# Retention and gated MLP on one core: w_in loaded by GpSimd with a cast, second w_sg transpose by DMA, state work moved to GpSimd

## The chip, the cores and the metric

The kernel runs on one core of one Trainium2 chip. TensorE (PE) does the matmuls; its weight loads (PEld) overlap them. VectorE (DVE), ScalarE (ACT) and GpSimd (POOL) work element by element, and SyncE (SP) issues DMAs. The metric is the device time of the core in microseconds, as a median of several runs. Most executions of one kernel agree within 0.3%.

## The reference

Eight heads of retention over a batch of 8, a sequence of 576 and a head size of 64, and on their output a gated MLP with a spatial gate:

```python
scores = scale * np.matmul(q, k.transpose(0, 1, 3, 2))
Dmat = np.where(rel >= 0, gamma[:, None, None] ** rel[None, :, :], 0.0)
x = np.matmul(scores * Dmat, v)            # then heads side by side: [8, 576, 512]
h = gelu_tanh(x @ w_in)                    # 512 x 1024
u, v = h[..., :512], h[..., 512:]
v_n = (v - mean(v)) / np.sqrt(var(v) + 1e-06) * g_ln
v_s = np.einsum('ts,bsd->btd', w_sg, v_n) + b_sg[None, :, None]
out = x + (u * v_s) @ w_out
```

Inputs and output are float32; the kernel's matmuls are in bfloat16.

## The kernel before, in words

Two batch rows of 576 positions make nine tiles of 128; four such pairs make N = 36 units. A unit is 256 positions of four heads, or, for the middle one of each nine (MID), 64 positions of both rows and all heads. For a unit, q, k and v are loaded (`load`, L288 and L280), scaled by powers of gamma and cast (`transposed`: q L484, k L478 or L480, v L487), q and k are transposed on PE (L500) or, from unit 24, by DMA, and copied out as qkT (L503). The scores (`score`, L525) are masked with a triangle on DVE (`mask`, L539, table `tri`), and multiplied with v (`outp`, L638).

Instead of scores over the whole past, a state of each head is carried. `states` (L558) makes the products of k and v of a unit's two chunks; `keep` copies them from PSUM (L585), adds the first chunk to the state (s1, L607, DVE), the second (s2, L614, DVE), and spreads both over the diagonal blocks of zbdB (L611, ACT) and zbdA (L590, POOL in the first four units, then DVE). `outp` multiplies those with q (L630). Up to unit 8 (JOIN) a unit's states and scores are an instruction group of their own, which takes the PSUM tile "oz"; after that they are joined with the output of the unit before. PSUM has the pools "tp", "s", "oz" and "d", the last with three banks that the MLP's products, the transposes of w_sg and the filler matmuls share.

The MLP follows the units: `mlp_V` (L702) the v half with w_in, then gelu (L705), statistics on DVE (L710 to L712), the power of -1/2 on POOL (L715), and the normalised tile vn (L727, ACT). `mlp_U` (L742) is the u half, transposed. When a batch row's tiles are complete, `batch` multiplies vn with the transposed w_sg (L764), gates on DVE (L772), multiplies by w_out (L784), adds x on PE (L787), and stores (L791, L793). The transposed w_sg exists twice, as wT0 for even rows of the batch and wT1 for odd ones, whose rows are shifted by half a tile. Free rows of their half-filled tiles carry b_sg, and those of vmid 1/g, split into two bfloat16 each (`g_and_b`).

Weights: w_in goes by SP in four loads of float32 into `wst`, and ACT casts it in eight pieces (`w_load`, L301, L305). w_sg is cast by POOL (L419), transposed on PE ten times (L428) and copied out by DVE and ACT (L437, L435). w_out is loaded (L443) and scaled by g on DVE (L446).

The order of the work is computed when the program is built. Every piece is added with `plan.add(engine, cost, key, ...)`; for each engine, the class `Plan` emits of the pieces that are ready by its own reckoning the one with the smallest key. A key is a due time (unit number times T0 = 5300) plus a correction from the table SHIFT, by engine, name of the tile and stage. On the chip each engine and each DMA queue then runs its list in that order, each piece behind its semaphores. Where PE would be idle in the first 45 us of that reckoning, `fill` puts in matmuls with zeros (L267).

Of the kernel before, what the change touches and what calls it, by code (L numbers as in the profile page):

```python
# [11 lines left out]
F32 = mybir.dt.float32  # L12
# [14 lines left out]
    "ACT xT late": 9412, "ACT xT mid": -23216, "ACT zbd late": -5690, "ACT zbd mid": 6227, "ACT zbdB e1": 8971,  # L27
    "ACT zbdB e2": 3443, "ACT zbdB e3": -2224, "ACT zbdB e5": 3662, "ACT zbdB e6": 1034, "ACT zbdB late": -8232,
    "ACT zbdB mid": 2910, "ACT zc e0": -5530, "ACT zc e2": -2593, "ACT zc e3": -15140, "ACT zc e6": 4358,
    "ACT zc late": 1898, "ACT zc mid": 4282, "ACT zmid e4": -40267, "ACT zmid late": 5855, "DVE b_rows e-2": 20418,  # L30
    "DVE b_rows e2": 8415, "DVE dtab e-2": -10349, "DVE gT e6": -9934, "DVE gT late": 4844, "DVE gT mid": -35727,
    "DVE g_col1 e2": 31456, "DVE g_rows e-2": -2310, "DVE qkT e0": 1726, "DVE qkT e1": 7061, "DVE qkT e3": 13460,
    "DVE qkT e4": -10701, "DVE qkT e5": -9864, "DVE qkT e6": -228, "DVE qkT late": 9156, "DVE qkT mid": 18488,
    "DVE qs e0": -234, "DVE qs e1": 24362, "DVE qs e3": 6022, "DVE ret e0": 703, "DVE ret e1": 1576,
    "DVE ret e2": 5275, "DVE ret e3": 8812, "DVE ret e4": 3411, "DVE ret e6": 6523, "DVE ret late": 7318,
# [5 lines left out]
    "DVE st3 e6": 1761, "DVE st3 late": -8207, "DVE st3 mid": -22642, "DVE vmid_g e2": 6581, "DVE wT e3": -5068,  # L41
    "DVE wT e5": -5845, "DVE wT_b e2": -3449, "DVE w_out e3": -15568, "DVE w_out e5": 25437, "DVE zbdA e4": -1133,
    "DVE zbdA e5": -5539, "DVE zbdA e6": -14755, "DVE zbdA late": -198, "DVE zbdA mid": -2512,
# [809 lines left out]
```

## Time and profile before

| | |
|---|---|
| median of 3 runs | 225.62 us (225.03 to 226.07) |
| profiled execution | 225.79 us |
| its span, first to last instruction | 223.4 us |
| mean granted TensorE clock | 0.998 |
| busy: PE, PEld | 206.5 us (92%), 143.4 us (64%) |
| busy: DVE, ACT, POOL | 172.6 us (77%), 156.3 us (70%), 120.0 us (54%) |
| DMA | 45.86 MB, mean 205 GB/s |
| matmuls with zeros (L267) | 36, 12.4 us |

Busy time counts matmuls of the filler too. An average over the span hides that the kernel has stages: an opening in which inputs and weights arrive, a long middle, and a tail in which the last outputs are made. A DMA share of 1 means that the 16 DMA engines always had packets under way. POOL's 54% hold long waits, since its list is in a fixed order.

### The profile page before, as it was taken

The page shows a single profiled execution, that of the slowest core. Times are in us where ns is not written, and L with a number is a line of the kernel's source. Part 1 is how long each engine was busy: PE and PEld are TensorE (multiplying, and loading weights), DVE is VectorE, ACT ScalarE, POOL GpSimd, SP SyncE. Part 2 cuts the span into 40 slices and gives each one's busy share as a digit, 9 for nine tenths or more (in the row PEclk, how much of TensorE's full clock was granted, in tenths as well). Part 3 has the DMA queues.
Part 4 walks back from the last instruction along what each step waited for, and adds up shares of the span by engine and source line. Part 5 has one row for each costly group of instructions (what it writes and reads, how often), then busy time and mean ns, then how long its engine had stood idle before and what let it go on. Part 6 is the DMA issues. An engine that isn't in the chain of part 4 may idle for free.

```text
span 223.4 us, 7695 instructions
## 1 busy us (share of the span) xinstructions
PE 206.5 (92%) x3085; PEld 143.4 (64%) x3122; DVE 172.6 (77%) x424; ACT 156.3 (70%) x351; POOL 120.0 (54%) x160
## 2 busy tenths in 40 slices
PE   4997879999998899999999998999989999999993
PEld 1454457677675676677767775677656766676751
DVE  5888587899998998769988997769889677665420
ACT  5276996936687558798577666895887678847432
POOL 4273559894788667485556476656767341002000
PEclk9999999999999999999999999999999999999999
DMA  4999899999899976879756999999889158300324
GB/s 91 284 311 188 260 285 308 269 335 294 176 293 305 321 196 179 243 216 301 242 147 208 229 200 198 221 264 204 218 186 224 53 50 175 112 1 0 144 94 188
DMA packets 84674, 45.86 MB, mean 205 GB/s; under 512 B 28768, under 2 KB 77920, under 8 KB 84640
## 3 DMA queue, kind: packets, MB, share of 16 engines
q1 hardware_dynamic: 84640, 45.38, 79.2%
q8 instruction: 24, 0.39, 0.8%
q14 instruction: 10, 0.08, 0.1%
HBM read 32.79 MB, written 9.44 MB: 189 GB/s over the span
## 4 chain that ended last, share of the span: by engine, by line
PE 68%; DVE 12%; DMA 7%; POOL 4%; ACT 4%; issue 3%; POOLq 0%; ACTq 0%
PE p_d L764 13%; PE p_d L784 12%; PE p_d L742 11%; PE p_d L702 10%; DMA qkf<-in_q_dram 6%; PE p_oz L638 4%; PE p_tp L500 3%; PE p_d L787 3%; PE p_s L525 3%; PE p_d L267 3%; DVE ret L539 2%; PE p_oz L630 2%; PE p_oz L558 2%; DVE s L607 2%; ACT xT L667 2%
## 5 line engine op out<-in xcount | busy, mean ns | idle before, releaser
L715 POOL TENSOR_TENSOR stat<-stat,mhalf 128x1 f32<-128x1 f32 x36 | 20.2, 561 | 55.0 <-DVE stat L712 45.0
L539 DVE TENSOR_TENSOR ret<-p_s,tri 128x512 bf16<-128x512 f32 x64 | 42.3, 684 | 8.1 <-PE p_s L525 8.1
L487 POOL TENSOR_TENSOR vb<-vf,gv 128x512 bf16<-128x512 f32 x36 | 39.0, 1084 | 9.8 <-DMA vf<-in_v_dram 6.5
L764 PE MATMUL p_d<-wT,vn 128*128 128x288 bf16 x256 | 41.1, 286 | 0.6 <-ACT vn L727 0.6
L742 PE MATMUL p_d<-xT,w_in 128*128 128x256 bf16 (+1 forms) x320 | 37.5, 262 | 2.0 <-ACT xT L667 1.9
L484 POOL TENSOR_TENSOR qkb<-qkf,gq 128x512 bf16<-128x512 f32 x32 | 34.7, 1085 | 5.2 <-issue 4.9
L727 ACT ACTIVATE vn<-vg,stat 128x512 bf16<-128x512 f32 x32 | 25.9, 812 | 16.3 <-DVE stat L717 15.8
L702 PE MATMUL p_d<-w_in,xT 128*128 128x512 bf16 x121 | 34.7, 380 | 2.6 <-ACT xT L667 0.8
L784 PE MATMUL p_d<-w_out,uT 128*128 128x512 bf16 x133 | 36.2, 379 | 0.7 <-issue 0.2
L772 DVE TENSOR_TENSOR uT<-p_d,uT 128x288 bf16<-128x288 f32 x64 | 28.4, 450 | 6.8 <-PE p_d L764 6.4
L742 PEld LDWEIGHTS <-w_in 128*128 128x128 bf16 x320 | 28.0, 98 | 8.3 <-issue 2.5
L710 DVE BATCH_NORM_STATS2 stat<-vg 128x6 f32<-128x512 f32 x36 | 24.7, 686 | 9.8 <-ACT vg L705 9.6
L764 PEld LDWEIGHTS <-vn 128*128 128x128 bf16 x256 | 24.5, 98 | 9.4 <-issue 1.1
L791 ACT ACTIVATE ob<-p_d 128x512 f32<-128x512 f32 x36 | 21.2, 593 | 12.7 <-PE p_d L787 11.9
L667 ACT ACTIVATE xT<-p_oz 128x256 bf16<-128x256 f32 x64 | 24.4, 456 | 4.9 <-PE p_d L742 2.6
L747 ACT ACTIVATE uT<-p_d 128x512 bf16<-128x512 f32 x36 | 21.5, 597 | 7.9 <-PE p_d L742 7.5
L480 POOL CAST qkb<-qkf 128x512 bf16<-128x512 f32 x32 | 21.1, 660 | 9.7 <-issue 4.2
L705 ACT ACTIVATE vg<-p_d 128x512 f32<-128x512 f32 x36 | 21.3, 593 | 4.5 <-PE p_d L702 3.9
L702 PEld LDWEIGHTS <-xT 128*128 128x128 bf16 x144 | 12.5, 98 | 12.1 <-ACT xT L667 1.3
L784 PEld LDWEIGHTS <-uT 128*128 128x128 bf16 x144 | 13.3, 98 | 10.5
L764 PE MATMUL p_d<-wT,vmid 128*128 128x288 bf16 x64 | 18.3, 286 | 0.8 <-DVE uT L772 0.8
L611 ACT ACTIVATE zbdB<-s 64x128 bf16<-64x128 f32 x48 | 14.7, 306 | 6.2 <-DVE s L607 5.5
(87 smaller groups left out, 322.5 us busy)
## 6 DMA issues: line engine op xcount, KB each, us to landing
out_dram<-ob SPq DMA_DIRECT2D x36, 256.0 KB, 3.2
qkf<-in_q_dram SPq DMA_DIRECT2D x32, 256.0 KB, 5.0
qkf<-in_k_dram SPq DMA_DIRECT2D x32, 256.0 KB, 5.1
vf<-in_v_dram SPq DMA_DIRECT2D x32, 256.0 KB, 5.1
wst<-in_moe_w_in_dram SPq DMA_DIRECT2D x4, 512.0 KB, 5.8
wsg<-in_moe_w_sg_dram SPq DMA_DIRECT2D x4, 288.0 KB, 7.2
qkf<-in_q_dram SPq DMA_DIRECT2D x8, 128.0 KB, 5.1
qkf<-in_k_dram SPq DMA_DIRECT2D x8, 128.0 KB, 4.8
```

Source lines behind the costliest of these rows:

```text
L484: plan.add("DVE" if soon else "POOL", 640 if soon else 1030, key, lambda: eng.tensor_tensor(split(qs[a]), shape(qkf[l][:, 0, :]), gain(gq) ...
L487: plan.add("POOL", 1030, key + 2, lambda: nc.gpsimd.tensor_tensor(shape(vb[a][:]), shape(vf[l][:]), gain(gv), op=Alu.mult), reads=rd(i, 2) ...
L539: nc.vector.tensor_tensor(ret[r][hh][:].rearrange("p (s k j) -> p s k j", s=2, k=2), banks[0][:].rearrange("p (s k) j -> p s k j", s=2), t ...
L667: nc.scalar.activation(xT[p % NX][:, 2 * c:2 * c + 2, 128 * (m + e):128 * (m + e) + 128].rearrange("p k (j s) -> p k s j", s=2), oz[:, e, ...
L702: nc.tensor.matmul(banks[0][:], xT[p % NX][:, kk, 128 * m:128 * m + 128], w_in[:, kk, F2:], start=(kk == 0), stop=(kk == KK - 1))
L710: nc.vector.bn_stats(st[:, 0:6], vg[g][:])
L727: nc.scalar.activation(vn[p % 2][m][:], vg[g][:], Act.Identity, scale=st[:, 8:9], bias=st[:, 9:10])
L742: nc.tensor.matmul(hu[:, c, :], w_in[:, kk, 128 * (x * per + c):128 * (x * per + c) + 128], xT[p % NX][:, kk, cols], start=(kk == 0), stop ...
L747: plan.add("ACT", 500, key, lambda banks, x=x: nc.scalar.activation(uT[p % NX][:, x * per:x * per + per, cols], banks[0][:].rearrange("p ( ...
L764: nc.tensor.matmul(banks[0][:, :HS], src[:, 128 * c:128 * c + 128], wT[e][j][:, half * HS:(half + 1) * HS], start=(j == 0), stop=(j == SB ...
L772: plan.add("DVE", 370, key, lambda banks, c=c, col=col: nc.vector.tensor_tensor(uT[x][:, c, col:col + HS], banks[0][:, :HS], uT[x][:, c, c ...
L784: nc.tensor.matmul(banks[0][:], uT[x][:, c, r], w_out[:, c, :], start=(c == 0), stop=False, skip_group_check=True)
```

## The change

- **w_in**: `w_load` now issues four DMAs from GpSimd's queue that cast on the way and write the bfloat16 tile. Two stand behind vb of unit 0, the v half's, two behind vb of unit 1. The four loads on SP, the staging tiles (two are left, for w_out) and ACT's eight casts go.
- **g and b**: their three small loads and the work on them get later keys. GpSimd's constants are split: the ramp first, the identity, then the triangle (`pool_c`), on which the masks now wait instead of on the identity.
- **wT1**: PE transposes w_sg once, five tiles with five evacuations; wT1 is filled by two DMAs in SBUF, half the partitions each, from wT0, after all five tiles. The second batch row's products wait on them.
- **State**: s2 and all of zbdA but that of MID go to POOL. w_out is scaled on POOL too.
- **PSUM**: up to unit 8 the states take banks of "d", two where both chunks have a state, instead of "oz", and ACT copies each bank out by itself.
- **SHIFT** has new values throughout, so the order of the pieces changes in many places. In the planner a DMA of another engine than SP no longer holds that engine until the transfers before it are done.

```diff
@@ Plan.emit
             if dma:
-                free[e] = max(t + cost, pipe - 1000)
+                if e == "SP":
+                    free[e] = max(t + cost, pipe - 1000)
@@ w_load
-    def w_load(half, c, s):
-        plan.add("SP", 600, (-0.4 - 0.2 * half) * T0 + c,
-                 lambda: nc.sync.dma_start(wst[s][:], moe_w_in.rearrange("(c p) f -> p c f", p=128)
-                                           [:, c:c + 2, half * F2:(half + 1) * F2]),
-                 writes=[("wst", s)], dma=1900)
-        for r in range(2):
-            plan.add("ACT", 500, (1 + 0.4 * (1 - half)) * T0, lambda r=r: nc.scalar.activation(
-                w_in[:, c + r, half * F2:(half + 1) * F2], wst[s][:, r, :], Act.Copy),
-                reads=[("wst", s)], writes=[("w_in", half, c + r)])
+    def w_load(half, c):
+        plan.add("POOL", 900, (1 - half) * T0 + 10 + c, lambda: nc.gpsimd.dma_start(
+            w_in[:, c:c + 2, half * F2:(half + 1) * F2],
+            moe_w_in.rearrange("(c p) f -> p c f", p=128)[:, c:c + 2, half * F2:(half + 1) * F2]),
+            reads=[("vb", 1 - half)], writes=[("w_in", half, c), ("w_in", half, c + 1)], dma=1500)
@@ tables
-        plan.add("POOL", 200, early, pool_a, writes=["srow_i"])
-        plan.add("POOL", 1000, early + 1, pool_b, writes=["ident"])
+        plan.add("POOL", 350, early, pool_a, writes=["srow_i"])
+        plan.add("POOL", 600, early + 1e6, pool_b, writes=["ident"])
+        plan.add("POOL", 1500, early + 2e6, pool_c, writes=["tri"])
@@ g_and_b
-        plan.add("SP", 600, early + 1, lambda: nc.sync.dma_start(
+        plan.add("SP", 600, -2.9 * T0, lambda: nc.sync.dma_start(
             g_col[:], moe_g_ln.rearrange("(c p) -> p c", p=128)), writes=["g_col"], dma=300)
...
-        plan.add("SP", 900, early + 1, b_load, writes=["b_col"], dma=300)
+        plan.add("SP", 900, -2.9 * T0 + 1, b_load, writes=["b_col"], dma=300)
...
-        low = 2 * T0
+        low = 3 * T0
@@ weights
-        for e in range(2):
-            for j in range(SB):
...
+        for j in range(SB):
...
+        for x in range(2):
+            plan.add("SP", 600, kw + 2 * T0, lambda x=x: nc.sync.dma_start(
+                wTs[1][NB0:, :, :] if x == 0 else wTs[1][:NB0, 1:, :],
+                wTs[0][:NB0, :, :] if x == 0 else wTs[0][NB0:, :SB - 1, :]),
+                reads=[("wT", 0, j) for j in range(SB)], writes=[("wT1", x)], dma=1100)
...
-                plan.add("DVE", 450, kw + 1 * T0, lambda c=c, s=s, r=r: nc.vector.tensor_scalar(
+                plan.add("POOL", 620, kw + 1 * T0, lambda c=c, s=s, r=r: nc.gpsimd.tensor_scalar(
                     w_out[:, c + r, :], wst[s][:, r, :], g_col[:, c + r:c + r + 1], None, op0=Alu.mult),
@@ keep
+                for e, b in enumerate(banks):
+                    nc.scalar.activation(z[:, e].rearrange("p k d -> p (k d)"), b[:, :2 * D], Act.Copy)
...
-            plan.add("DVE", 220, key + 5, lambda: nc.vector.tensor_tensor(s2[c][:], z[:, 1], mid, op=Alu.add),
+            plan.add("POOL", 300, key + 5, lambda: nc.gpsimd.tensor_tensor(s2[c][:], z[:, 1], mid, op=Alu.add),
                      reads=[name, mid_name], writes=[("s2", c)])
             v = int(n > 1)
-            build("POOL" if i < 4 else "DVE", ("zbdA", c, v), zbdA[c][v], s2[c][:], [("s2", c)])
+            build("POOL", ("zbdA", c, v), zbdA[c][v], s2[c][:], [("s2", c)])
@@ attention
             def run(banks):
-                states(i, banks[0], 0, True)
-                score(i, banks[1:])
+                states(i, [banks[0], banks[w - 1]], True)
+                score(i, banks[w:])
             u = plan.add("PE", 470 if i % U == MID else 590, i * T0 + 3, run, reads=[("qkT", i % NR), ("kb", a), ("vb", a)],
-                         writes=[("sc", i), ("z", i)], take=[("oz", 1), ("s", 2)])
+                         writes=[("sc", i), ("z", i)], take=[("d", w), ("s", 2)])
@@ the order in which the pieces are added
-    for n, (half, c) in enumerate(((1, 0), (1, 2), (0, 0), (0, 2))):
-        w_load(half, c, n)
...
         attention(i)
+        if i < 2:
+            for c in (0, 2):
+                w_load(1 - i, c)
```

More of the change, by code (lines that the diff above doesn't have):

```diff
@@ L60 @@
-    "POOL zbdB late": 2130, "POOL zbdB mid": -3212, "SP b_col e-2": 12547, "SP g_col e-2": -9283,
-    "SP ld e0": -3117, "SP ld e1": -4642, "SP ld e2": 5103, "SP ld e3": -172, "SP ld e5": -1411, "SP ld e6": 5603,
-    "SP ld late": 11669, "SP ld mid": 1614, "SP out late": 2815, "SP out mid": 11693, "SP qkT late": -2778,
-    "SP qkT mid": -127, "SP wo e0": 24367, "SP wo e5": 3300, "SP wo e6": -1941, "SP wsg e0": -1456,
-    "SP wsg e1": 3613, "SP wsg e3": -5539, "SP wsg e4": -18215, "SP wst e-1": -392,
[7 rows of a table added]
@@ new lines @@
+    "POOL s2 e6": -10518, "POOL s2 late": -954, "POOL s2 mid": 4265, "POOL srow_i e-2": -24929, "POOL st2 e2": 765,
[3 rows of a table added]
+    "POOL w_in e0": 828, "POOL w_in e1": 4002, "POOL w_out e5": -4332, "POOL wnat e2": 6035, "POOL wnat e4": 6803,
+    "POOL zbdA e0": -1437, "POOL zbdA e1": -8927, "POOL zbdA e2": -5148, "POOL zbdA e3": -1976,
+    "POOL zbdA e5": -6423, "POOL zbdA e6": 3401, "POOL zbdA late": -4447, "POOL zbdA mid": -4628,
+    "POOL zbdB e0": 5300, "POOL zbdB e1": 93, "POOL zbdB e2": 4275, "POOL zbdB e5": -773, "POOL zbdB late": 2130,
[6 rows of a table added]
@@ L238 @@
     ob = [sb(f"ob{i}", [128, DM], F32) for i in range(NO)]
-    wst = [sb(f"wst{i}", [128, 2, F2], F32) for i in range(4)]
+    wst = [sb(f"wst{i}", [128, 2, F2], F32) for i in range(2)]
     w_in = sb("w_in", [128, KK, 2 * F2])
@@ new lines, in weights, with tr, put @@
+        for j in range(SB):
+            n = min(128, S - 128 * j)
+            def tr(banks, j=j, n=n):
+                for t in range(SB):
+                    w = min(128, S - 128 * t)
+                    nc.tensor.transpose(banks[0][:].bitcast(BF)[:n, 128 * t:128 * t + w],
+                                        wnat[:w, t, 128 * j:128 * j + n], ident[:w, :w])
+            u = plan.add("PE", 290, kw + 1 * T0, tr, reads=[("wnat", t) for t in range(SB)] + ["ident"],
+                         writes=[("wTp", j)], take=[("d", 1)])
+            def put(banks, j=j, n=n):
+                dst, src = wT[0][j][:n, :], banks[0][:].bitcast(BF)[:n, :S]
+                if j % 2:
+                    nc.scalar.activation(dst, src, Act.Copy)
+                else:
+                    nc.vector.tensor_copy(dst, src)
+            plan.add("ACT" if j % 2 else "DVE", 520 if j % 2 else 385, kw + 1 * T0, put,
+                     reads=[("wTp", j)], writes=[("wT", 0, j)], give=[(u, [0])])
@@ L641, in run @@
             if joined:
-                states(i + 1, oz, 2 * 128, False)
+                states(i + 1, [oz[:, e, 256:] for e in range(2)], False)
                 score(i + 1, banks[1:])
```

93 lines of the change are left out of this document (42 added, 51 removed), and 56 rows, old and new, of the table SHIFT.

## The prediction

> **What bounds the kernel now.** I read the page's head first, then busy time by stretch, then the same for the filler matmuls (L267), which do no work of the kernel. Columns: bounds in us, length, busy us (instructions) of PE, PEld, DVE, ACT, POOL, granted clock, DMA share, GB/s.
>
> ```profile
> span 223.4 us, 7695 instructions
> 0.00:20.00 20.00, 15.80 (x200) 7.93 (x204) 15.73 (x46) 10.29 (x35) 8.65 (x21) 1.00 0.94 233
> 20.00:35.00 15.00, 12.40 (x182) 7.69 (x182) 10.89 (x28) 14.01 (x28) 8.89 (x13) 1.00 0.91 253
> 35.00:45.00 10.00, 9.42 (x169) 6.85 (x168) 7.84 (x17) 8.46 (x17) 8.76 (x13) 1.00 1.04 279
> 45.00:80.00 35.00, 33.02 (x559) 24.28 (x563) 33.47 (x78) 23.14 (x56) 25.81 (x32) 1.00 1.06 289
> 80.00:210.00 130.00, 126.23 (x1913) 90.60 (x1936) 101.88 (x252) 96.82 (x212) 67.90 (x86) 1.00 0.72 174
> 210.00:223.40 13.40, 9.64 (x73) 6.08 (x72) 2.81 (x7) 3.58 (x6) 0.00 (x0) 0.96 0.38 144
> ```
> The fillers alone:
> ```profile
> 0.00:20.00 20.00, 9.70 (x27) 3.05 (x31) 1.00 0.94 233
> 20.00:35.00 15.00, 2.73 (x11) 0.61 (x8) 1.00 0.91 253
> ```
> PE's useful work is 6.1 us of the first 20, 9.7 of the next 15 and 9.4 of the next 10. From 80 to 210 us PE is busy 97%: there it is the bound, and little can be won but by giving it less to do. So the time is PE's work plus what PE loses: 13.9 us in 0:20, 5.3 in 20:35, 0.6 in 35:45, 2.0 in 45:80, 3.8 in 80:210, 3.8 in the tail. The change acts on the first three, and in 45:80, where DVE (96%), PE (94%) and the DMA engines are all near full at once.
>
> The opening by timeline (start, length):
> ```profile
> 0.80 0.45 SPq L362 DMA_DIRECT2D g_col<-in_moe_g_ln_dram  x1
> 1.31 0.49 SPq L367 DMA_DIRECT2D b_col<-in_moe_b_sg_dram  x1
> 1.85 0.56 SPq L368 DMA_DIRECT2D b_col<-in_moe_b_sg_dram  x1
> 2.46 0.58 SPq L288 DMA_DIRECT2D qkf<-in_q_dram  x1
> ...
> 11.82 1.34 SPq L301 DMA_DIRECT2D wst<-in_moe_w_in_dram  x2
> ...
> 13.72 1.38 POOL L487 TENSOR_TENSOR vb<-vf,gv 128x512 bf16<-128x512 f32 x1
> ...
> 16.37 5.58 SPq L280 DMA_DIRECT2D vf<-in_v_dram  x2
> 16.70 0.76 ACT L667 ACTIVATE xT<-p_oz 128x256 bf16<-128x256 f32 x2 [0.50 <-PE p_oz L638]
> ...
> 22.00 1.14 SPq L301 DMA_DIRECT2D wst<-in_moe_w_in_dram  x2
> 22.75 1.67 PE L702 MATMUL p_d<-w_in,xT 128*128 128x512 bf16 x7 [0.16 <-issue]
> ...
> 30.21 1.14 ACT L305 ACTIVATE w_in<-wst 128x512 bf16<-128x512 f32 x2
> 31.84 1.91 PE L742 MATMUL p_d<-xT,w_in 128*128 128x256 bf16 x16
> ```
> The first q load is the fourth DMA. xT of the first pair of units is there at 17.46, but the v half's matmuls (L702) begin at 22.75 and the u half's (L742) at 31.84, right behind ACT's casts of w_in. ACT is busy 14.01 of 15 us there. The MLP could have filled PE, and w_in was late.
>
> **The change, part by part.** Prices by shape (count | busy us, mean ns | idle before):
> ```profile
> L590 DVE TENSOR_TENSOR zbdA<-s,blk 128x256 bf16<-128x256 f32 x20 | 10.9, 546 | 0.3
> L590 POOL TENSOR_TENSOR zbdA<-s,blk 128x256 bf16<-128x256 f32 x4 | 2.7, 670 | 6.2 <-DVE s L614 6.2
> L614 DVE TENSOR_TENSOR s<-zc,s 128x128 f32<-128x128 f32 x16 | 8.3, 520 | 0.2
> L614 DVE TENSOR_TENSOR s<-zc 128x128 f32<-128x128 f32 x8 | 3.9, 492 | 0.0
> L484 POOL TENSOR_TENSOR qkb<-qkf,gq 128x512 bf16<-128x512 f32 x32 | 34.7, 1085 | 5.2 <-issue 4.9 <-DMA qkf<-in_q_dram 0.3
> L480 POOL CAST qkb<-qkf 128x512 bf16<-128x512 f32 x32 | 21.1, 660 | 9.7 <-issue 4.2 <-POOL stat L715 3.3 <-POOL qkb L484 2.2
> L446 DVE TENSOR_SCALAR w_out<-wst,g_col 128x512 bf16<-128x512 f32 x4 | 2.3, 596 | 0.0
> L305 ACT ACTIVATE w_in<-wst 128x512 bf16<-128x512 f32 x8 | 4.6, 619 | 0.0
> L585 ACT ACTIVATE zc<-p_oz 128x256 f32<-128x256 f32 x24 | 9.0, 374 | 3.0 <-PE p_oz L558 2.9
> L585 ACT ACTIVATE zc<-p_oz 128x128 f32<-128x128 f32 x8 | 2.2, 276 | 1.2 <-PE p_oz L558 1.1
> ```
>
> (a) Second transposed w_sg by DMA. Half of L428's transposes go. Their windows:
> ```profile
> 35.00:45.00 10.00, 4.72 (x49) 3.39 (x49) 1.00 1.04 279
> sum 45.00, PE 4.94 PEld 3.48; mean PE 2.47 PEld 1.74
> ```
> 25 of 50 leave PE: 2.5 us, in a stretch where PE has hardly a gap, so I count all of it. Five evacuations on DVE and ACT go too. Added are two copies in SBUF, 64 partitions each: 64 x 5 x 1152 B and 64 x 4 x 1152 B, 0.66 MB, which at the 289 GB/s of 45:80 is 2.3 us of DMA time in a full stretch. Batch 1 is their reader, some two units after batch 0, so their landing is covered; without that cover they cost a landing:
> ```profile
> vf<-in_v_dram SPq DMA_DIRECT2D x32, 256.0 KB, 5.1
> ```
> 5.1 us for a load. The two issues stand in SP's queue behind the wait for all five tiles; the loads queued behind wait with them. Bounds: 0 (fewer loads then needed at once) and 4.6 us (only half the partitions are written at a time, half rate). I take 1.2, nearer to the lower, because units are loaded up to five ahead.
>
> (b) g and b later. The first load moves from 2.46 to 0.80, 1.66 us, and everything that the DMA engines pace until 20 us moves with it (share 0.94). Bounds 0 and 1.66, the whole, since nothing else stands ahead of it; I take 1.7. The three issues (1.5 us) now stand between loads of SP's queue, where a pair of issues takes up to 5.58 us for lack of room; hidden there, else 1.5. GpSimd's ramp constant goes first and its triangle last; DVE's eight copies for g and b leave the way of the first q and land after 16 us, where 20:35 has 4.1 us of DVE idle: nothing either way.
>
> (c) w_in by four casting loads. ACT loses eight casts, 4.6 us, in its fullest stretch, and w_in no longer waits for them. The loads go out behind vb of units 0 and 1, some 8 to 11 us, ahead of where 11.82 and 22.00 were. PE lost 5.3 us in 20:35, so the gain is between 0 and 5.3, and I take half, 2.7: half a w_in (1.05 MB, 3.6 us at 289 GB/s) now flows beside the q, k and v of units 2 to 4 that used to flow after them, and delays those. POOL issues four DMAs: no row of before shows one. The nearest are SP's, 0.67 us for a w_in load (1.34 for two) and 2.8 for a blocked one: 2.7 to 11 us of POOL, the lower nearest as the rings are empty then; POOL is busy 8.65 of the first 20, which hides it. Behind them on POOL wait vb of unit 1 and zbdA; if uncovered they delay unit 1 by 1.3 us.
>
> (d) States into the "d" banks for units 0 to 8. PE does the same matmuls; ACT's one copy of 374 ns becomes two of 276 in six of them: 6 x 0.18 = 1.1 us, paid from the 4.6 it gains. What is late next: two of three "d" banks are held until those copies end, while "oz" is free for the output. Bounds: five units that meet MLP work x 0.55 = 2.8 lost, 0.37 x 5 = 1.9 won. I take 0.
>
> (e) s2, zbdA and w_out from DVE to POOL. DVE loses 8.3 + 3.9 + 10.9 + 2.3 = 25.4 us of 172.6. POOL gains 20 x 0.67 = 13.4; for s2 (128x128, no row) the line through 670 ns at 256 and 1085 at 512 columns gives 0.46, bounds 0.25 and 0.67, so 24 x 0.46 = 11.0; w_out has one streamed input, so nearer to the cast's 0.66 than to 1.09: 2.6 to 4.3. In 45:80:
> ```profile
> 45.00:80.00 35.00, 2.54 (x5) 1.00 1.06 289
> 45.00:80.00 35.00, 3.41 (x5) 0.00 (x0) 1.00 1.06 289
> ```
> Five L614 and five L590 by window: DVE falls by 2.54 + 3.41 + 2.30 = 8.3 to 25.2 of 35, POOL rises by 5 x 1.13 + 2.6 = 8.3 to 34.1. DVE's fullness goes and POOL's takes its place. PE lost 2.0 us there; I take neither gain nor loss, since the state products are wanted only two units later. The bounds are 2.0 won and the second rival's loss.
>
> The row has POOL at 670 ns against DVE's 546 for the same zbdA. The Trainium skill (GPSIMD Engine Reference, Engine selection) holds GpSimd to be about twice as slow for two-input elementwise work. By that, an estimate from DVE's rows, the ten products and sums would cost 5 x 2 x (0.55 + 0.51) = 10.6 instead of 5.7 us and POOL would need 39 of 35 us; the sum would come out near 224, the second rival's time. The four POOL rows speak against it, at 1.2 times.
>
> Sum against the profiled execution's 225.79 (span 223.40 and 2.39 around it): 2.5 - 1.2 + 1.7 + 2.7 = 5.7, so 220.1. That execution stands 0.17 over the median of 225.62; I say 220.0. Half a per cent, 1.1 us, is about what a measurement of this kernel can tell from no change, as its runs spread from 225.03 to 226.07.
>
> **The rivals.**
> First: the opening speeds up more. w_in early also brings statistics, gelu and batch 0 forward. PE loses 19.8 us before 45; with all of (b), all 5.3 of 20:35 and no price for the copies: 225.8 - 2.5 - 1.7 - 5.3 = 216.3. For it: POOL idles 11 of the first 20 us and ACT is freed. Against: the DMA share is 0.91 to 1.06 from the start, so loads cannot come much sooner.
>
> Second: POOL becomes the bound in 45:80. At 34.1 of 35 us it has no room for its waits:
> ```profile
> POOL stat L715 <- DVE stat L712: 45.0, 24, 9.0
> ```
> It waits 45 us over the run for DVE's statistics, in order, with q, k and v of later units queued behind, whose buffers gate SP's loads. If half of the 9.2 us it idles there cannot be used, 8.3 - 4.6 = 3.7 us goes on the path: 223.7. Against: DVE, which it waits for, becomes quicker.
>
> Third, slower: w_in starves the first units. The casting loads sit ahead of units 2 to 4 in the DMA engines. If a casting transfer holds them twice as long as a plain one (no row shows one), 2.1 MB costs 7.3 us more, before the MLP has anything to cover it: 227.3. It decides from 5.7 us extra, 1.8 times the plain transfer; slower by over half a per cent from 6.8. For it: share 0.94 in 0:20. Against: the transfer writes half the bytes. The Trainium skill (DMA: Bandwidth & Descriptors, Issuing engines are not separate DMA queues) says that queues of all engines end on the same 16 DMA engines and interleave; no run here has a second queue yet.
>
> Fourth: the change doesn't bite. DMA paces PE until 45 whatever is removed, the copies in SBUF eat what the transposes gave: 225.5.
>
> **How the numbers follow.** Forecast (217.5 to 222.5) 0.47; first rival 0.13; second 0.15; fourth 0.08; third 0.17. Faster: 0.47 + 0.13 + 0.15 = 0.75; within half a per cent 0.08; slower 0.17. The range reaches from the first rival's 216 to 225.5: it leaves out 0.17 and a little of the first rival.
>
> **What would show it.** (a) PE's transposes at 25, no evacuation into the second wT. (b) First q issue near 0.8. (c) L702's successor before 20 us and L742's before 26, fillers under 12.4 us (9.70 + 2.73); wrong if vb of unit 2 (POOL, 13.72 before) begins more than 3 us later. (d) No wait of PE for ACT's zc copies over a microsecond. (e) DVE under 150 us, POOL near 150; wrong if PE's lost time in 45:80 grows over 2 us. The whole fails if PE's useful work by 45 us stays near 25 us.

## The result, and the profile after

The changed kernel takes 230.40 us in the median (four runs, 230.32 to 231.16) beside 225.32 us for the kernel before (four runs, 224.21 to 226.07): a ratio of 1.0247, 95% interval 1.0213 to 1.0281. It is slower by 5.1 us, where 220.0 was forecast with a range to 225.5. The profiled execution took 230.45 us, with a span of 228.6. Ratios, here and below, leave out executions in the chip's slower state; medians are of all executions.

Line numbers of the changed kernel: L275 filler, L392 the subtraction in `b_split`, L412 its transposes on PE, L308 the casting loads of w_in, L458 w_out's scaling, L634 s2, L610 the diagonal blocks zbdA, L722 and L762 the v and u halves of the MLP, L784 the spatial products, L804 the output products.

Busy time by stretch after the change, with the columns of the prediction's first table, and below it the fillers alone:

```profile
0.00:20.00 20.00, 15.31 (x193) 7.37 (x193) 13.78 (x34) 11.27 (x38) 11.82 (x27) 1.00 1.03 231
20.00:35.00 15.00, 9.03 (x153) 5.69 (x155) 14.06 (x28) 6.60 (x17) 10.44 (x14) 0.86 0.82 224
35.00:45.00 10.00, 9.89 (x129) 7.10 (x130) 5.87 (x17) 7.51 (x13) 6.68 (x10) 0.88 1.02 255
45.00:80.00 35.00, 32.04 (x554) 23.19 (x554) 25.54 (x58) 23.90 (x60) 34.63 (x44) 1.00 0.91 230
80.00:210.00 130.00, 125.88 (x1957) 89.38 (x1955) 94.28 (x230) 97.60 (x211) 85.01 (x119) 1.00 0.78 187
210.00:228.60 18.60, 14.70 (x113) 9.34 (x110) 3.88 (x9) 6.67 (x11) 0.32 (x1) 1.00 0.38 142
```
```profile
0.00:20.00 20.00, 8.52 (x23) 2.34 (x23) 0.27 (x1) 1.00 1.03 231
20.00:35.00 15.00, 1.20 (x4) 0.27 (x4) 0.00 (x0) 0.86 0.82 224
```

PE's useful work by 45 us is 15.31 + 9.03 + 9.89 - 9.72 = 24.5 us, against 25.2 before: the sign that the prediction had named for its failure as a whole. And a part of those 24.5 us ran at a lower clock (0.86 and 0.88 instead of 1.00), so still less was done in them. POOL stands at 34.63 of 35 us in 45:80, and PE's lost time there grew from 2.0 to 3.0 us; DVE is busy 157.4 us, where under 150 was named. So two of the signs for (e) failed as well. The chain of work that ended last, in order of time (start, length, what), names three places:

```profile
27.52 4.40 DVE b_rows L392
...
55.66 1.55 POOL w_out L458
...
60.44 3.09 POOL w_out L458 x2
...
83.75 3.28 DVE zbdA L610 x2
```

**The first place, 27 to 37 us.** The timeline (start, length) of DVE, POOL and PE there:

```profile
27.25 0.23 DVE L391 CAST b_rows<-b_col 128x8 bf16<-128x8 f32 x1
27.52 4.39 DVE L392 TENSOR_TENSOR b_rows<-b_col,b_rows 128x8 bf16<-128x8 f32 x1
31.94 0.17 DVE L393 COPY b_rows<-b_rows 128x16 bf16<-128x16 bf16 x1
```
```profile
27.00 0.45 POOL L634 TENSOR_TENSOR s<-zc,s 128x128 f32<-128x128 f32 x1
27.39 0.66 POOL L426 CAST wnat<-wsg 64x576 bf16<-64x576 f32 x1
28.02 0.66 POOL L610 TENSOR_TENSOR zbdA<-s,blk 128x256 bf16<-128x256 f32 x1
28.64 1.05 POOL L496 TENSOR_TENSOR qkb<-qkf,gq 128x512 bf16<-128x512 f32 x1
29.64 0.60 POOL L492 CAST qkb<-qkf 128x512 bf16<-128x512 f32 x1
30.21 1.05 POOL L499 TENSOR_TENSOR vb<-vf,gv 128x512 bf16<-128x512 f32 x1
31.21 0.66 POOL L426 CAST wnat<-wsg 128x576 bf16<-128x576 f32 x1
```
```profile
27.44 0.29 PE L537 MATMUL p_s<-qkT 64*64 64x64 bf16 x14
32.17 0.77 PE L412 MATMUL p_d<-ident,b_rows 128*128 128x128 bf16 x5 [4.44 <-DVE b_rows L391]
```

A subtraction of eight columns, 0.18 us in the kernel before (at 5.28 us, with nothing beside it), is on DVE for 4.39 us: from 27.52 to 31.91 us, while POOL works through six instructions without a gap and ends at 31.87. PE's next instructions in order need b's rows and wait 4.44 us. An instruction of the moved work for g was held as well, though no wait of PE shows for it: L365, 0.16 us in the kernel before, is on DVE for 1.60 us, from 13.66 to 15.26, and POOL's run of work ends at 15.23. What follows is PE's clock (four-microsecond stretches; the clock is the third number from the end):

```profile
28.00:32.00 4.00, 0.00 (x0) 0.00 (x0) 3.97 (x2) 0.53 (x2) 3.87 (x6) 0.83 0.99 286
32.00:36.00 4.00, 3.83 (x33) 2.14 (x34) 3.30 (x11) 1.19 (x2) 0.00 (x0) 0.50 1.12 318
36.00:40.00 4.00, 4.00 (x33) 2.59 (x32) 1.48 (x7) 1.79 (x3) 1.77 (x3) 0.81 1.03 248
```

PE is busy 7.83 of the 8 us after the stop, at a clock of 0.50 and 0.81. In the kernel before it is 1.00 throughout the first 45 us. The Trainium skill (TensorE: Matmul & The Clock Gate, Part 1) has PE fall to half clock after an idle window of about 3.4 us; the 4.44 us here agree. In e_fill, below, it falls after a shorter stop too.

**The second place, 54 to 64 us.** Groups by shape (count | busy us, mean ns of one | idle before):

```profile
L458 POOL TENSOR_SCALAR w_out<-wst,g_col 128x512 bf16<-128x512 f32 x4 | 6.2, 1565 | 0.0
L492 POOL CAST qkb<-qkf 128x512 bf16<-128x512 f32 x32 | 19.4, 606 | 1.3 <-PE p_s L537 1.1 <-PE p_oz L570 0.2
L610 POOL TENSOR_TENSOR zbdA<-s,blk 128x256 bf16<-128x256 f32 x24 | 16.5, 687 | 0.4
L634 POOL TENSOR_TENSOR s<-zc 128x128 f32<-128x128 f32 x8 | 3.6, 452 | 0.3 <-ACT zc L601 0.2
L804 PE MATMUL p_d<-w_out,uT 128*128 128x512 bf16 x144 | 37.2, 379 | 2.2 <-POOL w_out L458 2.2
```

One scaling of w_out takes 1.57 us on POOL, 2.6 times DVE's 0.60 and 2.6 times a cast of the same shape on POOL. The four stand between q, k and v of later units, POOL has no room left, and PE waits 2.2 us for them.

**The third, at 83.75 us,** is DVE's pair of products of the middle unit. It takes 3.36 us from 83.66 us, beside POOL instructions without a gap until 86.41; the same pair takes 0.74 us at 33.14, where POOL stands still. PE waits 1.65 us behind it. So of the chain, 12.3 us stand in these three.

The rest of the opening went as forecast: the transposes (L433) are 25, the first q load is issued at 0.79 us, the v half begins at 14.23 instead of 22.75 us and the u half at 19.79 instead of 31.84. Only the fourth unit is later: its v lands at 20.7 instead of 16.2 us, with the casting loads of w_in under way from 7.4 to 20.9 us, and is prepared 7 us later (L499 at 23.38 instead of 16.33 us).

### The profile page after: what moved, and what is told of

It is laid out like the page before. It is cut to its first block, busy times and chain, and to the rows that moved or that the text cites. A ratio compares the mean times of both kernels' runs of the same rounds, so it can differ in the third digit from the quotient of the medians.

```text
span 228.6 us, 7635 instructions
## 1 busy us (share of the span) xinstructions
PE 206.8 (90%) x3085; PEld 142.1 (62%) x3085; DVE 157.4 (69%) x373; ACT 153.6 (67%) x347; POOL 148.9 (65%) x212
## 3 DMA queue, kind: packets, MB, share of 16 engines
q0 software_dynamic: 1088, 1.05, 2.8%
## 4 chain that ended last, share of the span: by engine, by line
PE 49%; DVE 19%; ACT 10%; POOL 9%; DMA 7%; issue 3%; SPq 0%; ACTq 0%; POOLq 0%
PE p_d L784 12%; PE p_d L722 9%; PE p_d L804 9%; PE p_d L762 8%; DVE ret L551 5%; DMA w_in<-in_moe_w_in_dram 4%; DVE stat L730 3%; PE p_oz L658 3%; POOL vb L499 2%; PE p_d L807 2%; DVE s L627 2%; ACT vg L725 2%; POOL w_out L458 2%; DVE zbdA L610 2%; DVE b_rows L392 2%
## 5 line engine op out<-in xcount | busy, mean ns | idle before, releaser
L499 POOL TENSOR_TENSOR vb<-vf,gv 128x512 bf16<-128x512 f32 x36 | 38.2, 1064 | 11.2 <-PE p_oz L658 8.1
L784 PE MATMUL p_d<-wT,vn 128*128 128x288 bf16 x256 | 41.0, 286 | 1.0 <-ACT wT L441 0.5
L762 PE MATMUL p_d<-xT,w_in 128*128 128x256 bf16 (+1 forms) x320 | 38.6, 266 | 2.3 <-DMA w_in<-in_moe_w_in_dram 0.8
L722 PE MATMUL p_d<-w_in,xT 128*128 128x512 bf16 x144 | 37.9, 388 | 3.0 <-DMA w_in<-in_moe_w_in_dram 1.9
L804 PE MATMUL p_d<-w_out,uT 128*128 128x512 bf16 x144 | 37.2, 379 | 2.2 <-POOL w_out L458 2.2
L496 POOL TENSOR_TENSOR qkb<-qkf,gq 128x512 bf16<-128x512 f32 x32 | 33.9, 1060 | 1.7 <-PE p_tp L512 1.3
L762 PEld LDWEIGHTS <-w_in 128*128 128x128 bf16 x320 | 28.4, 99 | 8.0 <-issue 2.1
L784 PEld LDWEIGHTS <-vn 128*128 128x128 bf16 x256 | 24.1, 98 | 10.5 <-issue 3.6
L687 ACT ACTIVATE xT<-p_oz 128x256 bf16<-128x256 f32 x64 | 24.5, 459 | 5.0 <-PE p_oz L658 3.9
L722 PEld LDWEIGHTS <-xT 128*128 128x128 bf16 x144 | 14.0, 100 | 14.3 <-issue 4.5
L804 PEld LDWEIGHTS <-uT 128*128 128x128 bf16 x144 | 12.8, 98 | 13.0 <-issue 2.6
L492 POOL CAST qkb<-qkf 128x512 bf16<-128x512 f32 x32 | 19.4, 606 | 1.3 <-PE p_s L537 1.1
L784 PE MATMUL p_d<-wT,vmid 128*128 128x288 bf16 x64 | 18.4, 287 | 1.7 <-DVE uT L792 1.7
```

The costliest lines, as they stand in the source:

```text
L496: plan.add("DVE" if soon else "POOL", 640 if soon else 1030, key, lambda: eng.tensor_tensor(split(qs[a]), shape(qkf[l][:, 0, :]), gain(gq) ...
L499: plan.add("POOL", 1030, key + 2, lambda: nc.gpsimd.tensor_tensor(shape(vb[a][:]), shape(vf[l][:]), gain(gv), op=Alu.mult), reads=rd(i, 2) ...
L687: nc.scalar.activation(xT[p % NX][:, 2 * c:2 * c + 2, 128 * (m + e):128 * (m + e) + 128].rearrange("p k (j s) -> p k s j", s=2), oz[:, e, ...
L722: nc.tensor.matmul(banks[0][:], xT[p % NX][:, kk, 128 * m:128 * m + 128], w_in[:, kk, F2:], start=(kk == 0), stop=(kk == KK - 1))
L762: nc.tensor.matmul(hu[:, c, :], w_in[:, kk, 128 * (x * per + c):128 * (x * per + c) + 128], xT[p % NX][:, kk, cols], start=(kk == 0), stop ...
L784: nc.tensor.matmul(banks[0][:, :HS], src[:, 128 * c:128 * c + 128], wT[e][j][:, half * HS:(half + 1) * HS], start=(j == 0), stop=(j == SB ...
```

## The experiments

Each keeps the order of the kernel it starts from, but for what it moves, unless "planned anew" stands beside it. Ratios are against the kernel before on the same chip; one per cent is 2.26 us. A difference of two ratios is good to about 0.6 to 1 per cent, since executions spread wider than the 0.3% named at the start: those of the kernel before from 224.07 to 227.66 us on one chip.

| run | median us | ratio to the kernel before, 95% interval |
|---|---|---|
| the changed kernel | 230.40 | 1.0247 [1.0213, 1.0281] |
| e_brow | 229.12 | 1.0121 [1.0058, 1.0185] |
| e_fill | 229.08 | 1.0129 [1.0082, 1.0177] |
| e_wout | 226.68 | 1.0055 [1.0022, 1.0087] |
| e_state | 233.73 | 1.0361 [1.0308, 1.0413] |
| e_brow_wout | 225.42 | 0.9986 [0.9951, 1.0022] |
| e_brow_wout_mid | 221.76 | 0.9838 [0.9779, 0.9897] |
| e_undo_b | 229.57 | 1.0185 [1.0134, 1.0235] |
| e_undo_c (planned anew) | 229.51 | 1.0195 [1.0142, 1.0248] |
| e_wnat_act | 228.14 | 1.0157 [1.0104, 1.0209] |
| e_best_undo_b | 221.34 | 0.9861 [0.9808, 0.9914] |
| e_best_undo_c (planned anew) | 224.05 | 0.9937 [0.9898, 0.9977] |
| e_best_undo_a (planned anew) | 228.35 | 1.0139 [1.0092, 1.0186] |
| e_best_again | 221.37 | 0.9817 [0.9733, 0.9901] |
| e_best_undo_a2 | 228.99 | 1.0107 [1.0023, 1.0191] |
| e_best_state | 229.92 | 1.0165 [1.0101, 1.0229] |
| e_best_wnat | 219.80 | 0.9729 [0.9668, 0.9790] |

The theory at the start: two separate losses, DVE's moved work held beside POOL (and PE's clock with it), and w_out on POOL. Rivals: one loss seen from two sides; w_in landing late; the state work on POOL. In the expectations, theory A is the held work, B is POOL's fullness from 45 to 80 us, and C is w_in landing late.

### The held subtraction: e_brow, e_fill

e_brow does b's subtraction on POOL, in its place:

```diff
-                    nc.vector.tensor_tensor(lo, x, hi, op=Alu.subtract)
+                    nc.gpsimd.tensor_tensor(lo, x, hi, op=Alu.subtract)
```

> The changed kernel with one edit: the subtraction that makes b's second bfloat16 part (L392, two inputs in SBUF) runs on POOL instead of DVE; the order on PE, ACT and SP is the same. Theory A, the lock: DVE's L392 took 4389 ns for work of some 180 because POOL ran without a gap from 27.0 to 31.9 us, PE had nothing for 4.4 us, and then a granted clock of 0.5 for about 5 us. Without it PE's gap at 28 us goes, the clock stays at 1.0, and the kernel takes 224 to 226 us (4.4 us of gap and up to 2 of slow clock). Theory B, POOL is the bound from 45 to 80 us: the opening's gain is taken back there, 228.5 to 230.5 us. Theory C, w_in lands late and holds the third unit: the gap is another wait in disguise, PE stands still at 28 us all the same, 229.5 to 230.5 us.

It took 0.21 us there, so its data had been in place. The ratio falls by 1.26 points, 2.8 us; the time, 229.12, lies in the range of theory B and above that of A. In the trace its gelus and outputs lead the changed kernel's by 1.0 us at 17 us, before the edit acts, by up to 5.8 us at 38 and by a constant 3.0 to 3.2 from 56 us on. The clock is 1.00 from 28 us on, and the 4.4 us stop is gone. But the hold itself went to the next DVE instruction with two inputs in SBUF:

```profile
29.57 3.70 DVE L610 TENSOR_TENSOR zbdA<-zmid,blk 128x256 bf16<-128x256 f32 x2
```
```profile
34.26 1.02 PE L722 MATMUL p_d<-w_in,xT 128*128 128x512 bf16 x4 [1.84 <-DVE wT L417]
```

e_fill keeps the hold and has PE do eleven matmuls with zeros in the gap:

```diff
         def b_tr(banks):
+            for _ in range(11):
+                fill(banks[0])
```

> The changed kernel with 11 filler matmuls of 379 ns ahead of the transposes of b on PE, where it stood still for 4.4 us. The wait stays, only the clock after it is kept up. Theory A: the slow clock has a price of its own; matmuls from 32 to 37 us run at 1.0 instead of 0.5, 1.5 to 2.5 us saved, 228 to 229 us. If the clock's drop has no price (other engines set the pace after the wait): 230 to 230.8 us. Theory B: no change either, 230 us.

PE's gap fell to 1.96 us, but the clock, which was to stay up, fell all the same: 0.57 in 32:36, with 1.00 in the stretches on either side. The trace's lead over the changed kernel was 0.7 us at 23 us, before the edit acts, 1.4 at 57 us and within 0.3 of nought from 67 us on; the median is 1.3 us lower, with runs from 227.86 to 230.31. The lead goes where the clock falls a second time: 0.70 in 64:68, behind two waits for w_out of 1.1 and 1.2 us, where the changed kernel has the same waits and 1.00. So the run doesn't give the clock a price of its own.

### w_out on POOL: e_wout, and both together: e_brow_wout

```diff
-                plan.add("POOL", 620, kw + 1 * T0, lambda c=c, s=s, r=r: nc.gpsimd.tensor_scalar(
+                plan.add("POOL", 620, kw + 1 * T0, lambda c=c, s=s, r=r: nc.vector.tensor_scalar(
                     w_out[:, c + r, :], wst[s][:, r, :], g_col[:, c + r:c + r + 1], None, op0=Alu.mult),
```

> The changed kernel with the four scalings of w_out back on DVE (596 ns each there before, 1565 ns on POOL now), at the same places of the order. Theory B: POOL, at 34.6 of 35 us in 45 to 80, gets 6.3 us back and PE does not wait 2.2 us for w_out at 62 us; 225.5 to 228 us. Theory A: the loss lies before 45 us and POOL's queue catches up later; 229.5 to 230.5 us.

1.92 points, 4.3 us. The lag against the changed kernel is nought to 60 us, -2 at 65 to 80 and -3.5 from 89 us on: the second and, POOL having room, the third place. One scaling took 0.69 us on DVE, in the mean.

> Both single undos at once: the subtraction of b on GpSimd and the four scalings of w_out back on DVE, the order on PE, ACT and SP as in the changed kernel. If the two are separate losses they add: 3.0 + 3.5 = 6.5 us off, about 224.0, half a per cent under the kernel before. If they are one loss seen from two sides (the opening's lag is caught up wherever GpSimd has room again), no more than the larger, 3.5 us, comes off: 226.9. If w_in's late landing holds the opening by itself, the same 226.9 and the lag against the changed kernel stays near nought until 60 us.

2.61 points, 5.9 us, where the two alone gave 2.8 and 4.3. The time lies between the cases for one loss (226.9) and for two (224.0), and the points are nearer to the sum than to the larger, within their doubt: so two losses for the most part. The version without them is level with the kernel before, and no better.

### The last hold: e_brow_wout_mid

The middle unit's products go to POOL as well:

```diff
-            e = nc.gpsimd if eng == "POOL" else nc.vector
+            e = nc.gpsimd
```

> The same, and the middle unit's two zbdA products (DVE, at 29.6 us held for 3.70 instead of 0.9) on GpSimd as well. If a DVE instruction is held only because it is of the kind that GpSimd's back-to-back work keeps out, the next one of that kind takes its place and nothing is won (224.0, give or take 0.5). If the two products were the last in the way, PE's 1.84 us at 34 us goes and a lock at 84 us with it: 222.0 to 223.0. Price: 1.4 us more on GpSimd per middle unit.

Another 1.5 points, 3.3 us: 221.76, and 221.37 when run again (e_best_again). No DVE instruction is longer than 1.7 us from 10 to 95 us, and in the profiled execution the clock is 1.00 in every stretch of the opening. The holds and w_out together cost the changed kernel 9.2 us by the ratios, 10.0 us by the traces' ends. Without them the change is faster than the kernel before by 1.6 to 1.8 per cent.

> The fastest version once more, to stand beside the three below: 221.8, within 1.2 us.

### Taking away what DVE waits for: e_wnat_act

Instead of moving the held instruction, five casts are taken from POOL:

```diff
-            plan.add("POOL", 575, kw, lambda j=j, n=n: nc.gpsimd.tensor_copy(wnat[:n, j, :], wsg[j][:n, :]), reads=[("wsg", j)], writes=[("wnat", j)])
+            plan.add("POOL", 575, kw, lambda j=j, n=n: nc.scalar.activation(wnat[:n, j, :], wsg[j][:n, :], Act.Copy), reads=[("wsg", j)], writes=[("wnat", j)])
```

> The changed kernel with the five float32-to-bfloat16 casts of w_sg on ACT (idle over 8 of 15 us there) instead of GpSimd, nothing moved on DVE. If DVE's subtraction of b is held for as long as GpSimd runs without a gap, taking two casts of 0.66 us out of that run shortens it from 4.39 to about 3.1 us, and the end comes 0.5 to 1.5 us earlier. If it waits for its data or for something on its own engine, it stays at 4.4 whatever GpSimd does.

The time fits the first case, a little beyond its 0.5 to 1.5 us: 0.9 points, 2.0 us. The trace fits neither. DVE and POOL:

```profile
28.20 0.98 DVE L392 TENSOR_TENSOR b_rows<-b_col,b_rows 128x8 bf16<-128x8 f32 x1
29.21 0.52 DVE L393 COPY b_rows<-b_rows 128x16 bf16<-128x16 bf16 x1
29.64 0.15 DVE L391 CAST b_rows<-b_col 64x2 bf16<-64x2 f32 x1
29.83 0.91 DVE L392 TENSOR_TENSOR b_rows<-b_col,b_rows 64x2 bf16<-64x2 f32 x1
```
```profile
28.09 1.05 POOL L496 TENSOR_TENSOR qkb<-qkf,gq 128x512 bf16<-128x512 f32 x1
29.09 0.61 POOL L492 CAST qkb<-qkf 128x512 bf16<-128x512 f32 x1
29.66 1.06 POOL L499 TENSOR_TENSOR vb<-vf,gv 128x512 bf16<-128x512 f32 x1
```

Each held instruction ends within 0.05 us of the end of one POOL instruction (29.18 beside 29.14, 29.73 beside 29.70, 30.74 beside 30.72), the first two with POOL still going on. So it is POOL that holds DVE, instruction by instruction; but why DVE gets in at each boundary here, and at none of five in the changed kernel, stays open.

The Trainium skill (SBUF — State Buffer, Who interferes with whom) names a port pair that the two engines share: a DVE instruction with two inputs in SBUF and a GpSimd instruction that reads SBUF exclude one another, and who has the pair keeps it for the whole instruction. It counts copies and casts, under conditions, among those that can contend. That agrees with this run, where the second held one is a copy, and with which instructions were held most (two SBUF inputs: b's subtraction, zbdA); in e_wout the held one was the cast ahead of the subtraction, at 3.94 us. The hold through six instructions goes beyond it.

### The parts undone: (b), (c), (a), the state

(b): the loads of g and b first again, their small DVE work ahead of the first q (`self.calls` is the planned order, collected before it is emitted); in the changed kernel, and in the version without holds.

```diff
+        first = [c for c in self.calls if c[1] in ("g_col", "b_col")]
+        split = [c for c in self.calls if c[1] in ("g_col1", "b_rows") and c[2].__name__ in ("g_split", "b_split")]
+        rest = [c for c in self.calls if c not in first + split]
+        at = max(n for n, c in enumerate(rest) if c[1] in ("b_rows", "g_rows", "srow")) + 1
+        self.calls = first + rest[:at] + split + rest[at:]
```

> The changed kernel with only the loads of g and b first in SP's queue again and their thirteen small DVE instructions ahead of the first q, everything else in its place. If the lock on the moved work is the loss, 3.0 us come off at least, and the 1.66 us of earlier first load that it gives up decide the rest: 227.4 if that lead was worth nothing by the end, 229.1 if it was worth all of it. If the moved work isn't the cause, the time grows by up to 1.7, to 232.

> The three moves of the fastest version so far (221.8 us), with the loads of g and b first in SP's queue and their small DVE work ahead of the first q; all else in its place. No lock is left to be relieved, so this prices the earlier first load alone. If the 1.66 us that I counted for it reach the end, 223.4; if PE catches them up behind the fillers, 221.8.

In the changed kernel 1.4 us off: the held pair is then the middle unit's, 3.21 us at 31 us. Without holds the undo makes no difference that can be told (221.34 beside 221.76). In the trace, beside e_brow_wout_mid's, the v half begins 3.4 us later (17.64 instead of 14.21), the first three gelus are 1.4 us later, and all from 53 us on 0.8: the version with the lead waits 1.86 us of it for w_in.

(c): w_in by SP and ACT as before, planned anew (`w_load` and `wst` of the kernel before).

> The changed kernel with w_in by SP's queue into four float32 buffers and eight ACT casts, as before; its order is planned anew, so about 1.5 us either way say nothing. If the casting loads bring the 2.7 us that I predicted, it is slower than the changed kernel: 233. If they hold the units behind them for more than they bring, it is faster: 227.5 to 229. First u half's matmul back from 19.8 to about 30 us in either case.

> The same version with w_in by SP's queue and ACT's casts as in the kernel before; order planned anew, about 1.5 us either way say nothing. If the casting loads bring the 2.7 us of my sum, 224.5. If they hold up the first units for as much as they bring, 221.8; if they cost more, under 220.5.

In the changed kernel the undo is 1.2 us faster, within the doubt of a new order; without holds it is slower by 1.0 point, 2.2 us. That is about what was forecast for the casting loads, but not much above the 1.5 us that a new order alone can bring.

(a): the transposes back on PE, first planned anew, then in place:

```diff
-            plan.add("SP", 600, kw + 2 * T0, lambda x=x: nc.sync.dma_start(
-                wTs[1][NB0:, :, :] if x == 0 else wTs[1][:NB0, 1:, :],
-                wTs[0][:NB0, :, :] if x == 0 else wTs[0][NB0:, :SB - 1, :]),
...
+            def tr1(banks, j=j, c0=c0, r0=r0):
+                for t in range(SB):
+                    w = min(128, S - 128 * t)
+                    nc.tensor.transpose(banks[0][:].bitcast(BF)[r0:128, 128 * t:128 * t + w],
+                                        wnat[:w, t, c0:c0 + 128 - r0], ident[:w, :w])
...
+            self.calls[at:at] = [("PE", "tr1", self.second[j][0], [banks]), ("", "put1", self.second[j][1], [banks])]
```

> The same version with the second transposed w_sg by 25 transposes on PE and five evacuations instead of the two copies by DMA; order planned anew, with the same 1.5 us of doubt. My sum has the copies worth 2.5 - 1.2 = 1.3 us: 223.1. If all of PE's 2.5 us counts and the copies are free, 224.3; if the copies' hold on SP's queue eats them, 221.8.

> The fastest version with 25 transposes and five evacuations in the place of the two copies by DMA, each behind the evacuation of the first w_sg's tile of the same number, all else in its planned place. My sum has this part at 1.3 us: 223.1. If PE's 2.5 us count in full, 224.3; if the copies' place in SP's queue costs as much, 221.8. If the 6.6 us of the run planned anew belong to the transposes and not to that run's order, 228.

228.35 and 228.99: 6.8 and 6.5 us, far above every value of my sum for the transposes. The order planned anew had its own loss (PE busy 1.66 of 5 us at 50:55, clock 0.50 behind it), the one in place shows where the rest comes from:

```profile
38.52 0.98 PE L449 MATMUL p_d<-ident,wnat 128*128 128x128 bf16 x10 [0.55 <-DVE wT L477]
...
40.70 0.53 PE L449 MATMUL p_d<-ident,wnat 128*64 128x128 bf16 x5 [0.74 <-ACT wT L475]
...
42.60 0.75 PE L469 MATMUL p_d<-ident,wnat 128*128 128x128 bf16 x5 [0.35 <-DVE wT L459]
...
46.19 1.12 PE L814 MATMUL p_d<-wT,vn 128*128 128x288 bf16 x4 [0.74 <-ACT wT L475]
```

Its gelus stand 1.6 us behind at 33 us and 7.4 us behind from 51 us to the end. PE does 25 transposes more (2.5 us), waits for their evacuations in gaps of 0.35 to 0.74 us, and its clock is 0.82, 0.50 and 0.83 in the stretches from 40 to 52 us: 3.4 us of full clock missing there. How much of it belongs to the one order that I wrote can't be told; two orders agree on the sum. The kernel before, whose order was made for all fifty transposes, had 0.1 us of such waits in all.

The state: s2 and the zbdA of units 4 and up on DVE again, in the changed kernel (shown) and in the version without holds (there the middle unit's stay on POOL).

```diff
-            e = nc.gpsimd if eng == "POOL" else nc.vector
+            e = nc.gpsimd if eng == "POOL" and i < 4 else nc.vector
...
-            plan.add("POOL", 300, key + 5, lambda: nc.gpsimd.tensor_tensor(s2[c][:], z[:, 1], mid, op=Alu.add),
+            plan.add("POOL", 300, key + 5, lambda: nc.vector.tensor_tensor(s2[c][:], z[:, 1], mid, op=Alu.add),
```

> The changed kernel with s2 and, from unit 4, zbdA back on DVE at the same places of the order. POOL loses 24 x 0.46 and 20 x 0.67, some 24 us. In 20 to 35 POOL loses s2 at 27.0 (0.45) alone and the lock of DVE's L392 remains. Theory B: POOL was the bound in 45 to 80; 226 to 228.5 us. Theory A: the opening's gap remains, and DVE is full again in 45 to 80 as it was before the change; 229.5 to 231.5 us.

> The fastest version with the state's second sum and the diagonal blocks of units 4 and up on DVE again (the middle unit's stay on GpSimd). My sum took this move as worth 0: 221.8. Undoing it in the changed kernel cost 3.3 us, growing from 100 us to the end: 225 if that was the state work itself; if it was DVE instructions meeting GpSimd's there, 221.8 to 223 here.

2.6 and 7.8 us slower, both above every case that I had named. Here are the second sum's rows of the last run; on POOL, in e_best_again, the same two take 472 and 454 ns:

```profile
L634 DVE TENSOR_TENSOR s<-zc,s 128x128 f32<-128x128 f32 x16 | 6.5, 404 | 0.0
L634 DVE TENSOR_TENSOR s<-zc 128x128 f32<-128x128 f32 x8 | 5.8, 722 | 0.0
```

Over all 24 that is 0.51 us on DVE and 0.47 on POOL, so the sums themselves are hardly slower, though single ones take from 0.27 to 1.13 us on DVE. The lag grows from 2.1 us at 53 us to 10.2 at 180; PE is busy 114.1 instead of 117.4 of the 120 us from 80 to 200 us, DVE 93.6 instead of 83.7, and ACT's normalised tiles wait 9.5 instead of 3.1 us for DVE's statistics. Which of DVE's waits carries the loss to PE isn't shown.

These undone parts sum to far more than the 4 us between the two versions, so none is a price against the kernel before, whose order had been made for them. Of the same 120 us PE lost 5.9 in e_best_state, but 3.7 in the kernel before, with the state on DVE too, and 2.6 in e_best_again.

### Both ideas together: e_best_wnat

No long holds, and w_sg's casts on ACT.

> The fastest version with the five casts of w_sg on ACT too, which took 2 us off the changed kernel. No lock is left for them to lengthen, so they should be worth under 0.7 us here, on either side: 221.1 to 222.5. If GpSimd's fullness in 20 to 45 us still delays PE, up to 2 us off: 220.

219.80 us (219.54 to 220.40), ratio 0.9729. The spans of the two profiles differ by 0.2 us only (217.8 and 218.0) and the intervals overlap, so its lead over e_best_again (1.6 us in the medians) is not shown. PE in 45:80 is at 33.81 us, POOL at 31.64.

## Why the prediction was wrong, by its steps

**(b), the step that failed first.** "DVE's eight copies for g and b ... land after 16 us, where 20:35 has 4.1 us of DVE idle: nothing either way." I counted DVE's idle time and not what stands beside it, and called copies what are thirteen small instructions, five of them with two inputs. One of these instructions was held for 4.39 us, and PE had no work in its order that could pass it. e_brow prices this at 2.8 us, the whole chain of holds with the middle unit's at some 6. The trace of before had warned of it, though not with this work, which ran there at 5 us with POOL quiet. I had quoted a mean of 0.52 us for the second sum. The same shape takes 0.28 us there with POOL standing still, and 1.37 us beside a cast and a product of POOL:

```profile
12.60 0.28 DVE L614 TENSOR_TENSOR s<-zc 128x128 f32<-128x128 f32 x1
37.66 1.37 DVE L607 TENSOR_TENSOR s<-zc,zmid 128x128 f32<-128x128 f32 x1
```

I did not ask on what it depends. The earlier first load, counted at 1.7 us, was worth nothing measurable at the end.

**(e), w_out.** "w_out has one streamed input, so nearer to the cast's 0.66 than to 1.09: 2.6 to 4.3." One scaling took 1.57 us, above both bounds, 6.3 us for the four, where I took 2.6 and at most 4.3. That helped to bring POOL to 34.63 us (34.1 forecast) and PE to a wait of 2.2 us. e_wout has it at 4.3 us. This is the second rival in its place and nearly its price (3.7), but by one mis-sized instruction instead of the waits on statistics, so the nearness is luck; I had given it 0.15.

**(e), the state.** The prices were right (0.452 and 0.473 for 0.46, 0.687 for 0.67, DVE in 45:80 25.5 for 25.2). The worth, counted at nothing, is not settled: undone in the version without holds it costs 7.8 us, about half of the lag growing in 80:210, which I had held to be PE's alone. But in the kernel before, in its own order, PE lost only 3.8 of those 130 us, and in the version without holds 2.6 and 1.2 in the two profiles.

**(a).** 2.5 us of PE left, as counted, and the copies' landing (8.8 and 9.2 us) shows in none of PE's waits, so the 1.2 us that I took off for them don't show. The 6.5 us of the undo are the price in an order made without these transposes, and not what they cost in the kernel before.

**(c).** Right in mechanism: the v and u halves began as forecast. The size, 2.2 us in the version where nothing undoes it, for 2.7, is near, but from an order planned anew. POOL's issue of a load took 0.79 us for 0.67. The third rival's doubled transfer is refuted: the queue of the casting loads,

```profile
q0 software_dynamic: 1088, 1.05, 2.8%
```

used 2.8% of 228.6 us, 6.4 us for 2.1 MB read and 1.05 MB written, less than the 7.3 that I had for a plain transfer. What is left of that rival are PE's waits for w_in, 1.9 us for L722 and 0.8 for L762, and the fourth unit's v, 4.5 us later in landing.

**(d)** was not tried by itself; no wait of PE for the zc copies over a microsecond shows, as forecast.

With b's subtraction, the middle unit's products and w_out's scaling each on the other engine the change gives 221.8 and 221.4 us, inside the range. Four stretches of e_best_again, and below them its fillers:

```profile
0.00:20.00 20.00, 14.61 (x191) 7.17 (x193) 15.31 (x39) 12.08 (x39) 12.36 (x28) 1.00 1.01 227
20.00:35.00 15.00, 12.37 (x206) 9.14 (x208) 11.29 (x29) 9.30 (x22) 13.14 (x20) 1.00 0.84 232
35.00:45.00 10.00, 8.34 (x155) 6.37 (x157) 8.02 (x18) 6.68 (x16) 9.63 (x14) 1.00 1.07 300
80.00:210.00 130.00, 127.36 (x1903) 91.11 (x1912) 87.33 (x219) 97.28 (x209) 81.47 (x115) 1.00 0.74 180
```
```profile
0.00:20.00 20.00, 7.36 (x21) 2.22 (x23) 0.27 (x1) 1.00 1.01 227
20.00:35.00 15.00, 0.98 (x3) 0.27 (x4) 0.00 (x0) 1.00 0.84 232
```

PE's lost time before 45 us, its idle time and the fillers, is 18.0 us here and 18.6 in e_brow_wout_mid, for 19.8 in the kernel before. That is 1.2 to 1.8 us of the 4.4 that the sum had for (b) and (c) in the opening. The rest of what this version wins lies in the transposes that PE no longer does and in 80:210, where the sum had nothing; the two profiles don't divide it more closely. So the total comes near the forecast in part by luck.

The changed kernel lost 9 us in two things: DVE's small work, two-input instructions above all, beside a POOL that has no pause, and one instruction on POOL priced by the wrong neighbour.

## What to carry to other kernels

Before work is moved, look at what runs on the neighbour engine at its new place: idle time of DVE beside a POOL that works without a gap is not free, for two-input instructions above all, and a tiny one in PE's path can cost PE the wait and then the clock. Price an operation on POOL by the same operation there (a scaling by a column is not a cast), and where none is in the trace keep the upper bound well above the nearest row. A part that is undone in an order made for it shows what it carries in that order, not its gain over the kernel before.

## What was not expected of the hardware

- A DVE instruction of 0.18 us stood for 4.39 us beside six POOL instructions without a gap; others for 3.94, and in pairs for 3.70, 3.36 and 3.21. In e_wnat_act they got in at the end of one POOL instruction each. Why once and not the other time is open.
- A scaling of 128x512 float32 by a column into bfloat16 took 1.57 us on POOL, a cast of the same tile 0.61, a two-input product 1.06.
- PE's clock fell without a long stop too: to 0.57 in 32:36 of e_fill, after a stop of 1.96 us, and to 0.61 in 28:32 of e_best_undo_a2, where PE was busy 3.42 of the 4 us and no stop before was longer than 1.3 us. It also differs between executions of one kernel. Of the ten of the version without holds (e_brow_wout_mid and e_best_again) the five at a mean clock of 0.998 or more took 219.85 to 220.78 us, and the five at 0.991 or less 222.11 to 224.58. By the idle window of the Trainium skill's page on TensorE only the fall after the 4.44 us stop would be expected; what else lowers the clock isn't known from these runs.
